# A segment-recurrent attention kernel: mask of the last keys only, token mask by a GpSimd multiply, row sums and selection in 32-column tiles, output projection whole

## The chip, the cores and the metric

One core of one Trainium2 chip. The metric is the device time of one execution in microseconds (us).

## The reference, cut to what matters

The kernel computes `g * a + (1 - g) * b`: `b` is a small MLP that fills gaps and plays no part here, `a` is attention over 64 segments of 32 tokens, each with 8 memory rows that come out of the segment before. That recurrence makes the 64 segments a chain.

```python
M, seg, H, Dh = 8, 32, 32, 128            # memory rows, tokens, heads, head size
idx = jnp.arange(M + seg)
mask = (idx[:, None] < M) | (idx[:, None] >= idx[None, :])   # memory rows see all, token rows are causal
mem = mem0                                                  # [1, 8, 512]
for s in range(64):
    h = concatenate([mem, x[:, 32*s:32*s+32]], axis=1)
    q, k, v = h@Wq, h@Wk, h@Wv                              # per head
    p = softmax(where(mask, q@k.T * scale, -1e9))
    o = (p @ v) @ Wo
    mem = o[:, :M]                                          # goes into the next segment
    outs.append(o[:, M:])
```

Of the kernel before, what the change touches and what calls it, by code (L numbers as in the profile page):

```python
# [23 lines left out]
def kernel(ctx, tc, A_x, A_mem0, A_Wq, A_Wk, A_Wv, A_Wo, A_seg_len, B_x, B_w1, B_b1, B_w2, B_b2, gate_w, out):  # L24
# [46 lines left out]
    MkA = l0.tile([P, 4, EW], BF16)  # L71
# [83 lines left out]
    nc.gpsimd.memset(MkA[:], 0.0)  # L155
    for hh in range(4):
        for g in range(4):
            q = slice(32 * g, 32 * g + 32)
            for (c0, c1) in ((0, M), (EW - LEFT, EW)):
                sl = MkA[q, hh, c0:c1]  # L160
                nc.gpsimd.affine_select(out=sl, in_=sl, pattern=[[0, c1 - c0]], compare_op=ALU.is_ge,
                                        fill=MASK_NEG, base=-LEFT * hh, channel_multiplier=1)
            sl = MkA[q, hh, 0:M]
            nc.gpsimd.affine_select(out=sl, in_=sl, pattern=[[0, M]], compare_op=ALU.is_ge,
                                    fill=MASK_NEG, base=LEFT * hh + LEFT - 1, channel_multiplier=-1)

            sl = MkA[q, hh, EW - LEFT:EW]
            nc.gpsimd.affine_select(out=sl, in_=sl, pattern=[[1, LEFT]], compare_op=ALU.is_ge,
                                    fill=MASK_NEG, base=LEFT * hh, channel_multiplier=-1)

            sl = MkA[q, hh, 2 * M:2 * M + RIDE]
            nc.gpsimd.affine_select(out=sl, in_=sl, pattern=[[1, RIDE]], compare_op=ALU.is_ge,
                                    fill=MASK_NEG, base=M, channel_multiplier=-1)
# [181 lines left out]

    def mask_mm():

        B = bank(7, [P, 512])
        S = B[:, 0:NG * EW].rearrange("p (i e) -> p i e", e=EW)
        nc.tensor.matmul(S, lhsT=ident[:], rhs=MkA[:].unsqueeze(2).to_broadcast([P, 4, 2, EW]),  # L360
                         start=True, stop=True, skip_group_check=True)
        return B, S
# [234 lines left out]
    def run_fill(n):  # L597
        for _ in range(n):
            next(fill, None)
# [21 lines left out]
    for s in range(nseg + 2):  # L621
# [11 lines left out]
        if live:  # L633
            B, S = S_next
            na, nb, nc_, nd, ne = ring
            ring = (nd, ne, na, nc_, nb)
# [28 lines left out]
            for kc in range(1, KC):  # L665
# [5 lines left out]
            nc.scalar.activation(out=E[:, :, 16:EW], in_=S[:, :, 16:EW], func=ACTF.Exp, scale=scale, accum_out=hist[:, s, 1:2])  # L671
            sm = bank(nc_, [P, NG, 8])
            nc.tensor.matmul(sm[:], lhsT=BO[:], rhs=E[:, :, 8:16], start=True, stop=False)  # L673
            nc.tensor.matmul(sm[:], lhsT=BO[:], rhs=E[:, :, 0:8], start=False, stop=True)  # L674
# [4 lines left out]
            nc.vector.tensor_tensor(out=Pm[:].rearrange("p i (a q) -> p i a q", q=8), in0=E[:, :, 0:16].rearrange("p i (a q) -> p i a q", q=8),  # L679
                                    in1=R[:, 0:8 * NG].rearrange("p (i q) -> p i q", q=8).unsqueeze(2).to_broadcast([P, NG, 2, 8]), op=ALU.mult)  # L680
# [3 lines left out]
            nc.tensor.matmul(sr, lhsT=BO[:], rhs=E[:, :, 16:48], start=True, stop=False, skip_group_check=True)  # L684
            nc.tensor.matmul(sr[:, :, 24:32], lhsT=BO[:], rhs=E[:, :, 48:56], start=False, stop=True, skip_group_check=True)
# [4 lines left out]
            run_fill(1)  # L690
        else:
            if s == nseg:
                ux_out(s - 2)
                x_mul(s - 1)
                av_x(s - 1, (ne, na, nc_, 7))
# [5 lines left out]
        for half in range(2):  # L701
            d = slice(256 * half, 256 * half + 256)
            wp = bank((nb, nd)[half], [P, 256])
            for u in range(8):
                wo_unit(wp, UTT[Tp % 2], 24 - 8 * sp, u, 256 * half, 256 * half + 256)
            if half == 0:
                flush(act_q, 2)
            (nc.scalar.copy if half else nc.vector.tensor_copy)(out=wsb[:, d], in_=wp[:])  # L708
# [4 lines left out]
        if live and s >= 1:  # L713
            av_x(s - 1, (ne, na, nc_, nb))
        run_fill(2 * (si == 3))
        if s + 1 < nseg:
            aT = S_next[0][:, NG * EW:NG * EW + KC * M].rearrange("p (k m) -> p k m", m=M)
            for m in range(KC):
                nc.tensor.matmul(aT[:, m, :], lhsT=wsb[:, m * P:(m + 1) * P], rhs=Sel[:, 0:M], start=False, stop=True, skip_group_check=True)  # L719
# [145 lines left out]
```

## The kernel before: the parts that the change and the argument touch

Four segments ("quarters" 0 to 3, `si` in the code) share one 128-row tile of x. A segment has 40 keys: 8 memory rows and 24 tokens fill 32 partitions, and the last 8 tokens are handled as a "left" part for a whole tile at once (`KL`, `VL`, `GL`). The scores of all 32 heads lie in one PSUM bank, 32 partitions for each of four heads.

```python
def mask_mm():                       # adds the mask to the scores' bank ahead of them: 448 columns
    B = bank(7, [P, 512])
    S = B[:, 0:NG * EW].rearrange("p (i e) -> p i e", e=EW)
    nc.tensor.matmul(S, lhsT=ident[:], rhs=MkA[:].unsqueeze(2).to_broadcast([P, 4, 2, EW]), start=True, stop=True, ...)
    return B, S

def prep_h(s): nc.gpsimd.tensor_copy(out=hT[s % NHT][:, :, M:32], in_=xTs[T][...])       # 96 columns
def prep_q(s): nc.gpsimd.tensor_copy(out=QT[:, :, 32:40], in_=QL[T % 2][...])            # 256 columns
def left_v_in(T): nc.gpsimd.tensor_copy(out=VL[T % 2][:], in_=vls.pop(T)[:])             # 1024 columns
def x_mul(s): ...                    # GpSimd: Px = E * R (token rows), racc += R; waits for the second reciprocal

for s in range(nseg + 2):
    if si == 3 and T + 1 < NT: left_v_in(T + 1)
    if si == 3 and T + 2 < NT: x_left(T + 2)              # GL, a GpSimd copy
    ...
    if s + 1 < nseg: prep_h(s + 1)
    if s >= 1:
        prep_q(s)
        x_mul(s - 1)
    # ... projections Q, K, V of this segment (L211, L222), scores ...
    nc.scalar.activation(out=E[:, :, 0:16], in_=S[:, :, 0:16], func=ACTF.Exp, ...)        # memory rows' columns
    nc.scalar.activation(out=E[:, :, 16:EW], in_=S[:, :, 16:EW], func=ACTF.Exp, ...)      # token rows' columns
    sm = bank(nc_, [P, NG, 8])
    nc.tensor.matmul(sm[:], lhsT=BO[:], rhs=E[:, :, 8:16], start=True, stop=False)        # sums, memory rows
    nc.tensor.matmul(sm[:], lhsT=BO[:], rhs=E[:, :, 0:8], start=False, stop=True)
    run_fill(5 + (si == 3))                                                               # side work on TensorE
    nc.vector.reciprocal(out=R[...], in_=sm[:])
    nc.vector.tensor_tensor(out=Pm..., in0=E[:, :, 0:16]..., in1=R..., op=ALU.mult)       # 128 elements
    av(Um, 8, s, V, Pm, 8, 0, 0)                                                          # value product, memory rows
    # ... sums of the token rows (L684, L685), their reciprocal (1.76 us), UTT casts, run_fill(1) ...
    for half in range(2):                                                                 # output projection
        wp = bank((nb, nd)[half], [P, 256])
        for u in range(8):
            wo_unit(wp, UTT[Tp % 2], 24 - 8 * sp, u, 256 * half, 256 * half + 256)
        (nc.scalar.copy if half else nc.vector.tensor_copy)(out=wsb[:, d], in_=wp[:])
    S_next = mask_mm()
    av_x(s - 1, (ne, na, nc_, nb))                                                        # value product, token rows of s-1
    run_fill(2 * (si == 3))
    for m in range(KC):                                                                   # selection of the new memory
        nc.tensor.matmul(aT[:, m, :], lhsT=wsb[:, m * P:(m + 1) * P], rhs=Sel[:, 0:M], start=False, stop=True, ...)
    nc.vector.tensor_copy(out=hn[:, :, 0:M], in_=aT)                                      # memory of the next segment
```

A scheduler may move instructions, but each engine runs its own in one order. The GpSimd copies of `prep_h`, `prep_q`, `left_v_in` and `x_left` stand, in program order, behind everything that the segment before put on GpSimd.

## Time and profile before

| | before |
|---|---|
| time, median of 4 runs | 835.51 us (835.13 to 835.79) |
| loop, first to last memory-row sums | 705.9 us |
| length of a segment, quarters 0 to 3 (medians) | 10.943, 10.996, 11.032, 11.681 us |
| TensorE weight-shape changes in 106 to 811 us | 574, some nine a segment |

A segment's length is taken from the start of its memory-row sums to the next segment's. I read the starts of matmuls throughout, since their ends are modelled and overlap. The waits of TensorE have the columns total us, how many, the longest:

```profile
PEld L384 <- DVE Pm L679: 32.0, 64, 1.6
```

The weight loads of the memory rows' value product wait for the VectorE multiply `Pm`, 64 times, 0.5 us each. PEld is only the loader; most of this lies beside the side matmuls, so it is a figure to compare and not time lost.

### The profile page before, as it was taken

The numbers are of one execution on the slowest core, as the hardware profiler recorded it, in microseconds if no ns is written. First come the engines' busy times: TensorE is split into PE (matmuls) and PEld (weight loads), VectorE is DVE, ScalarE is ACT, GpSimd is POOL, SyncE is SP. The second block draws the span as 40 slices with busy tenths as digits, with TensorE's granted clock in tenths as the row PEclk, the third lists the DMA queues.
The fourth block names the chain that finished last, engine by engine and source line by source line (L and its number), as shares of the span: only waits on it lengthen the run. The fifth ranks groups of instructions, "written<-read, shape, count | busy, mean of one in ns | idle before, by whom it ended". The sixth has DMA issues, their size and how long they took to land.

```text
span 832.9 us, 49239 instructions
## 1 busy us (share of the span) xinstructions
PE 804.7 (97%) x22405; PEld 495.4 (59%) x22417; DVE 501.7 (60%) x1019; ACT 434.0 (52%) x1245; POOL 273.7 (33%) x625
## 2 busy tenths in 40 slices
PE   6999999999999999999999999999999999999886
PEld 4665555665666665566566556656656656665554
DVE  5764256565666566666656565656656665666553
ACT  3555544555455555555554555455555555555552
POOL 8000234242424333332424242434243243424220
PEclk9999999999999999999999999999999999999999
DMA  9791210100000010101010100000010101010000
GB/s 318 253 391 44 87 32 7 28 12 24 15 23 23 17 28 10 37 11 35 10 27 13 35 11 22 23 20 26 12 34 10 36 10 35 5 35 5 10 5 24
DMA packets 38216, 37.64 MB, mean 45 GB/s; under 512 B 13545, under 2 KB 36434, under 8 KB 36466
## 3 DMA queue, kind: packets, MB, share of 16 engines
q1 hardware_dynamic: 37874, 34.31, 12.4%
q8 instruction: 177, 2.90, 1.5%
q14 instruction: 37, 0.30, 0.1%
q0 software_dynamic: 128, 0.13, 0.1%
HBM read 26.03 MB, written 6.29 MB: 39 GB/s over the span
## 4 chain that ended last, share of the span: by engine, by line
PE 93%; DVE 3%; DMA 1%; issue 1%; SPq 1%; ACT 1%; DVEq 0%; ACTq 0%
PE b L211 35%; PE b L233 18%; PE b L222 17%; PE b L384 5%; PE hp L456 4%; PE bp L473 4%; PE b L360 2%; PE b L369 2%; PE b L684 2%; PE b L719 1%; PE b L389 1%; PE b L673 1%; DMA Wo_sb<-in_A_x_dram 1%; PE b L320 1%; PE b L373 0%
## 5 line engine op out<-in xcount | busy, mean ns | idle before, releaser
L217 DVE STREAM_TRANSPOSE Tt<-b 128x512 f32<-128x512 f32 (+1 forms) x384 | 225.6, 613 | 85.5 <-PE b L211 71.8
L211 PEld LDWEIGHTS <-hT 128*32 128x32 bf16 x5120 | 134.7, 97 | 100.0 <-DVE hT L720 15.4
L233 PE MATMUL b<-Wo_sb,UTT 128*32 128x256 bf16 (+1 forms) x4736 | 162.7, 285 | 1.2 <-ACT UTT L619 0.8
L222 PE MATMUL b<-Wv_sb,hT 128*32 128x512 bf16 x2048 | 141.9, 379 | 0.0
L211 PE MATMUL b<-Wq_sb,hT 128*32 128x512 bf16 x2048 | 132.9, 380 | 1.4 <-DVE hT L720 1.4
L211 PE MATMUL b<-Wk_sb,hT 128*32 128x256 bf16 (+1 forms) x3072 | 133.3, 308 | 0.0
L233 PEld LDWEIGHTS <-UTT 128*32 128x32 bf16 x4736 | 121.4, 97 | 19.1 <-ACT UTT L619 1.5
L654 ACT CAST KT<-Tt 128x256 bf16<-128x256 f32 (+1 forms) x192 | 87.1, 476 | 53.6 <-DVE Tt L217 53.6
L605 POOL TENSOR_TENSOR Px<-E,R 128x256 bf16<-128x256 bf16 x64 | 43.0, 672 | 218.7 <-DVE R L689 218.7
L689 DVE RECIPROCAL R<-b 128x256 f32<-128x256 f32 x64 | 112.5, 1757 | 0.0
L654 POOL CAST QT<-Tt 128x512 bf16<-128x512 f32 x64 | 39.1, 611 | 192.6 <-DVE Tt L217 192.6
L619 ACT CAST UTT<-b 128x256 bf16<-128x256 f32 x256 | 76.8, 387 | 23.9 <-PE b L389 23.4
L708 ACT CAST wsb<-b 128x256 bf16<-128x256 f32 x66 | 24.6, 372 | 120.1 <-PE b L233 120.1
L677 DVE RECIPROCAL R<-b 128x64 f32<-128x64 f32 x64 | 35.6, 557 | 79.4 <-PE b L674 79.4
L654 ACT CAST QT<-Tt 128x512 bf16<-128x512 f32 x64 | 39.6, 619 | 66.7 <-DVE Tt L217 66.7
L384 PEld LDWEIGHTS <-V 32*128 32x128 bf16 x4096 | 35.3, 91 | 46.2 <-DVE Pm L679 32.0
L222 PEld LDWEIGHTS <-hT 128*32 128x32 bf16 x2048 | 49.5, 96 | 21.1
L688 ACT CAST UTT<-b 128x64 bf16<-128x64 f32 x128 | 20.9, 215 | 75.2 <-PE b L389 75.2
L461 ACT ACTIVATE hg<-hp,b_sb 128x256 bf16<-128x256 f32 x80 | 37.7, 473 | 38.9 <-PE hp L456 38.9
L456 PE MATMUL hp<-yT,w_sb 128*128 128x256 bf16 (+1 forms) x352 | 53.8, 278 | 2.8 <-ACT hg L461 1.5
L607 POOL TENSOR_TENSOR racc<-racc,R 128x320 f32<-128x320 f32 x64 | 55.5, 867 | 0.0
L720 DVE CAST hT<-b 128x32 bf16<-128x32 f32 x63 | 12.1, 191 | 62.4 <-PE b L719 61.6
(116 smaller groups left out, 1075.2 us busy)
## 6 DMA issues: line engine op xcount, KB each, us to landing
Wv_sb<-in_A_Wv_dram SPq DMA_DIRECT2D x4, 1024.0 KB
Wq_sb<-in_A_Wq_dram SPq DMA_DIRECT2D x4, 1024.0 KB
Wk_sb<-in_A_Wk_dram SPq DMA_DIRECT2D x4, 1024.0 KB
Wo_sb<-in_A_Wo_dram SPq DMA_DIRECT2D x2, 2048.0 KB
vd<-vt SPq DMA_DIRECT2D x32, 128.0 KB
vs<-vd SPq DMA_DIRECT2D x256, 16.0 KB
out_dram<-o SPq DMA_DIRECT2D x16, 128.0 KB
Wo_sb<-in_A_x_dram SPq DMA_DIRECT2D x1, 1024.0 KB
```

The lines of the kernel that those rows point to most:

```text
L211: nc.tensor.matmul(bk[32 * j:32 * j + 32, 0:n], lhsT=G[:, kc, :], rhs=W5[t][:, kc, h0:h1, j, :], start=(kc == 0), stop=(kc == KC - 1), til ...
L217: nc.vector.transpose(out=Tt[:, 0:n], in_=bk[:, 0:n])
L222: nc.tensor.matmul(bk[32 * j:32 * j + 32, :], lhsT=G[:, kc, :], rhs=Wv5[:, kc, 4 * vb:4 * vb + 4, j, :], start=(kc == 0), stop=(kc == KC - ...
L233: nc.tensor.matmul(bk[32 * g:32 * g + 32, :], lhsT=ut[:, i, j, c0:c0 + 32], rhs=Wo_sb[:, 4 * i + j, d0:d1], start=(j == 0 and i < 4), stop ...
L384: nc.tensor.matmul(U[j][:, i, :], lhsT=V[q, i, :], rhs=Pt[q, i, c_main:c_main + n], start=(i == 0), stop=False, skip_group_check=True, til ...
L456: nc.tensor.matmul(hp[:rows, :], lhsT=w1_sb[:, kc, fc * P:fc * P + rows], rhs=yTs[blk][:, kc, :], start=(kc == 0), stop=(kc == KC - 1))
L461: nc.scalar.activation(out=hg_[:rows, :], in_=hp[:rows, :], func=ACTF.Gelu_apprx_tanh, bias=b1_sb[:rows, fc:fc + 1], scale=1.0)
L605: nc.gpsimd.tensor_tensor(out=Px[:, :, 0:32], in0=E[:, :, 16:48], in1=Rr, op=ALU.mult)
L607: nc.gpsimd.tensor_tensor(out=racc[:], in0=racc[:], in1=R[:], op=ALU.add)
L619: nc.scalar.copy(out=UTT[T % 2][:, :, j, c0 + M:c0 + 40], in_=U[:])
L654: (nc.gpsimd.tensor_copy if bi == 2 else nc.scalar.copy)(out=dst, in_=Tv)
L689: nc.vector.reciprocal(out=R[:, 8 * NG:].rearrange("p (i q) -> p i q", q=32), in_=sr)
```

## The change

The intent is to cut TensorE time: the mask matmul covers only the left keys (128 columns instead of 448), the causal mask of the tokens becomes a multiply of E by 0 and 1 on GpSimd, the 128-row sums and the selection become groups of four 32-column tiles (so that TensorE need not change shape between them and the projections), and the output projection runs in one piece of 512 columns, copied by ScalarE alone.

```diff
 def mask_mm():
-        nc.tensor.matmul(S, lhsT=ident[:], rhs=MkA[:].unsqueeze(2).to_broadcast([P, 4, 2, EW]), ...)
+        for j in range(4):
+            q = slice(32 * j, 32 * j + 32)
+            nc.tensor.matmul(S[q].rearrange("p i (a b) -> p i a b", b=LEFT)[:, :, 0:7:6, :], lhsT=ident[:, q], rhs=MkL[:],
+                             ..., tile_position=(0, 32 * j))
+    def sums(o, rhs, start, stop):
+        for j in range(4):
+            q = slice(32 * j, 32 * j + 32)
+            nc.tensor.matmul(o[q], lhsT=BO[:, q], rhs=rhs, start=start, stop=stop, ..., tile_position=(0, 32 * j))
+    def mem_out(aT, wsb):            # the selection, 16 matmuls instead of 4
+        for m in range(KC):
+            for c in range(4): ...   # 32 columns of wsb each, tile_position=(0, 32 * c)
# ... in the loop, after the two exp ...
+            Em = E[:, :, 16:16 + RIDE]
+            nc.gpsimd.tensor_tensor(out=Em, in0=Em, in1=Tri[:].unsqueeze(1).to_broadcast([P, NG, RIDE]), op=ALU.mult)
-            nc.tensor.matmul(sm[:], lhsT=BO[:], rhs=E[:, :, 8:16], start=True, stop=False)
-            nc.tensor.matmul(sm[:], lhsT=BO[:], rhs=E[:, :, 0:8], start=False, stop=True)
+            sums(sm, E[:, :, 8:16], True, False)
+            sums(sm, E[:, :, 0:8], False, True)
-            nc.vector.tensor_tensor(out=Pm..., in0=E[:, :, 0:16]..., in1=R..., op=ALU.mult)
+            for c in (8, 0):
+                nc.vector.tensor_tensor(out=Pm[:, :, c:c + 8], in0=E[:, :, c:c + 8], in1=R..., op=ALU.mult)
# ... token sums likewise by sums(); banks rotated by one; flush(act_q, 2), waiting ScalarE copies, ahead of the projection ...
-        for half in range(2):
-            ... 16 units of 256 columns, first half copied by VectorE, second by ScalarE
+        wp = bank(nb, [P, Dm])
+        for u in range(8):
+            wo_unit(wp, UTT[Tp % 2], 24 - 8 * sp, u)
+        nc.scalar.copy(out=wsb[:], in_=wp[:])
```

More of the change, by code (lines that the diff above doesn't have):

```diff
@@ L70 @@
     VL = [l0.tile([P, SPT, 2, Dh], BF16, name=f"VL{i}") for i in range(2)]
-    MkA = l0.tile([P, 4, EW], BF16)
+    MkL = l0.tile([P, NG, 2, LEFT], BF16)
+    Tri = l0.tile([P, RIDE], BF16)
     BO = l0.tile([P, P], BF16)
@@ L152 @@
         nc.gpsimd.tensor_copy(out=SelL[i][:, RIDE:32], in_=Sel[:, LEFT * (SPT - 1 - i):LEFT * (SPT - i)])
-    nc.gpsimd.memset(MkA[:], 0.0)
-    for hh in range(4):
+    nc.gpsimd.memset(Tri[:], 1.0)
+    for g in range(4):
+        q = slice(32 * g, 32 * g + 32)
+        nc.gpsimd.affine_select(out=Tri[q, :], in_=Tri[q, :], pattern=[[1, RIDE]], compare_op=ALU.is_ge,
+                                fill=0.0, base=M, channel_multiplier=-1)
+    nc.gpsimd.memset(MkL[:], 0.0)
+    for i in range(0, NG, 2):
+        hh = i // 2
         for g in range(4):
             q = slice(32 * g, 32 * g + 32)
-            for (c0, c1) in ((0, M), (EW - LEFT, EW)):
-                sl = MkA[q, hh, c0:c1]
-                nc.gpsimd.affine_select(out=sl, in_=sl, pattern=[[0, c1 - c0]], compare_op=ALU.is_ge,
+            for c in range(2):
+                sl = MkL[q, i, c, :]
+                nc.gpsimd.affine_select(out=sl, in_=sl, pattern=[[0, LEFT]], compare_op=ALU.is_ge,
                                         fill=MASK_NEG, base=-LEFT * hh, channel_multiplier=1)
-            sl = MkA[q, hh, 0:M]
-            nc.gpsimd.affine_select(out=sl, in_=sl, pattern=[[0, M]], compare_op=ALU.is_ge,
+            sl = MkL[q, i, 0, :]
+            nc.gpsimd.affine_select(out=sl, in_=sl, pattern=[[0, LEFT]], compare_op=ALU.is_ge,
                                     fill=MASK_NEG, base=LEFT * hh + LEFT - 1, channel_multiplier=-1)
-            sl = MkA[q, hh, EW - LEFT:EW]
+            sl = MkL[q, i, 1, :]
             nc.gpsimd.affine_select(out=sl, in_=sl, pattern=[[1, LEFT]], compare_op=ALU.is_ge,
                                     fill=MASK_NEG, base=LEFT * hh, channel_multiplier=-1)
-            sl = MkA[q, hh, 2 * M:2 * M + RIDE]
-            nc.gpsimd.affine_select(out=sl, in_=sl, pattern=[[1, RIDE]], compare_op=ALU.is_ge,
-                                    fill=MASK_NEG, base=M, channel_multiplier=-1)
+        nc.gpsimd.tensor_copy(out=MkL[:, i + 1, :, :], in_=MkL[:, i, :, :])
     pools.update(nTt=2, nside=1)
@@ L354, in prep_q @@
         nc.gpsimd.tensor_copy(out=QT[:, :, 32:40], in_=QL[T % 2][:, :, LEFT * si:LEFT * si + LEFT])
+    def sums(o, rhs, start, stop):
+        for j in range(4):
+            q = slice(32 * j, 32 * j + 32)
+            nc.tensor.matmul(o[q], lhsT=BO[:, q], rhs=rhs, start=start, stop=stop, skip_group_check=True, tile_position=(0, 32 * j))
+    def mem_out(aT, wsb):
+        for m in range(KC):
+            for c in range(4):
+                nc.tensor.matmul(aT[32 * c:32 * c + 32, m, :], lhsT=wsb[:, m * P + 32 * c:m * P + 32 * c + 32], rhs=Sel[:, 0:M],
+                                 start=False, stop=True, skip_group_check=True, tile_position=(0, 32 * c))
     def mask_mm():
@@ L359, in mask_mm @@
         S = B[:, 0:NG * EW].rearrange("p (i e) -> p i e", e=EW)
-        nc.tensor.matmul(S, lhsT=ident[:], rhs=MkA[:].unsqueeze(2).to_broadcast([P, 4, 2, EW]),
-                         start=True, stop=True, skip_group_check=True)
+        for j in range(4):
+            q = slice(32 * j, 32 * j + 32)
+            nc.tensor.matmul(S[q].rearrange("p i (a b) -> p i a b", b=LEFT)[:, :, 0:7:6, :], lhsT=ident[:, q], rhs=MkL[:],
+                             start=True, stop=True, skip_group_check=True, tile_position=(0, 32 * j))
         return B, S
@@ L635 @@
             na, nb, nc_, nd, ne = ring
-            ring = (nd, ne, na, nc_, nb)
+            ring = (nb, nd, ne, na, nc_)
             qk_banks = (na, nb, nc_, nd, ne)
@@ L678 @@
             Pm = cw.tile([P, NG, 16], BF16, tag="Pm", bufs=1, name="Pm")
-            nc.vector.tensor_tensor(out=Pm[:].rearrange("p i (a q) -> p i a q", q=8), in0=E[:, :, 0:16].rearrange("p i (a q) -> p i a q", q=8),
-                                    in1=R[:, 0:8 * NG].rearrange("p (i q) -> p i q", q=8).unsqueeze(2).to_broadcast([P, NG, 2, 8]), op=ALU.mult)
+            for c in (8, 0):
+                nc.vector.tensor_tensor(out=Pm[:, :, c:c + 8], in0=E[:, :, c:c + 8], in1=R[:, 0:8 * NG].rearrange("p (i q) -> p i q", q=8), op=ALU.mult)
             Um = [bank(k, [P, NG, 8]) for k in (nd, ne, na, nc_)]
@@ L683 @@
             sr = B[:, 0:NG * 32].rearrange("p (i q) -> p i q", q=32)
-            nc.tensor.matmul(sr, lhsT=BO[:], rhs=E[:, :, 16:48], start=True, stop=False, skip_group_check=True)
-            nc.tensor.matmul(sr[:, :, 24:32], lhsT=BO[:], rhs=E[:, :, 48:56], start=False, stop=True, skip_group_check=True)
+            sums(sr, E[:, :, 16:48], True, False)
+            sums(sr[:, :, 24:32], E[:, :, 48:56], False, True)
             Tp, sp = divmod(s - 2, SPT)
@@ L690 @@
             run_fill(1)
+            flush(act_q, 2)
         else:
@@ L694 @@
                 x_mul(s - 1)
-                av_x(s - 1, (ne, na, nc_, 7))
+                av_x(s - 1, (nd, ne, na, nc_))
             else:
@@ L700 @@
         wsb = cw.tile([P, Dm], BF16, tag="wsb", bufs=9, name="wsb")
-        for half in range(2):
-            d = slice(256 * half, 256 * half + 256)
-            wp = bank((nb, nd)[half], [P, 256])
-            for u in range(8):
-                wo_unit(wp, UTT[Tp % 2], 24 - 8 * sp, u, 256 * half, 256 * half + 256)
-            if half == 0:
-                flush(act_q, 2)
-            (nc.scalar.copy if half else nc.vector.tensor_copy)(out=wsb[:, d], in_=wp[:])
+        wp = bank(nb, [P, Dm])
+        for u in range(8):
+            wo_unit(wp, UTT[Tp % 2], 24 - 8 * sp, u)
+        nc.scalar.copy(out=wsb[:], in_=wp[:])
         if s >= 2:
@@ L713 @@
         if live and s >= 1:
-            av_x(s - 1, (ne, na, nc_, nb))
+            av_x(s - 1, (nd, ne, na, nc_))
         run_fill(2 * (si == 3))
@@ L717 @@
             aT = S_next[0][:, NG * EW:NG * EW + KC * M].rearrange("p (k m) -> p k m", m=M)
-            for m in range(KC):
-                nc.tensor.matmul(aT[:, m, :], lhsT=wsb[:, m * P:(m + 1) * P], rhs=Sel[:, 0:M], start=False, stop=True, skip_group_check=True)
+            mem_out(aT, wsb)
             nc.vector.tensor_copy(out=hn[:, :, 0:M], in_=aT)
```

## The prediction

> **What bounds the kernel now.** I read the page's busy shares first, then its chain, then one segment in order of time. There are 64 segments of 32 tokens. Four of them (called quarters 0 to 3) share one 128-row tile of x.
>
> ```profile
> PE 804.7 (97%) x22405; PEld 495.4 (59%) x22417; DVE 501.7 (60%) x1019; ACT 434.0 (52%) x1245; POOL 273.7 (33%) x625
> PE 93%; DVE 3%; DMA 1%; issue 1%; SPq 1%; ACT 1%; DVEq 0%; ACTq 0%
> ```
>
> TensorE is busy 97% of the span and is 93% of the chain that ended last. In the loop (106 to 811 us) it stands for anything else less than 10 us. So a saving must be a saving of TensorE time, and what it saves it keeps only if no other engine makes it wait. The loop in order of time, TensorE only, in a quarter 0 (start, length):
>
> ```profile
> 509.32 0.82 PE L222 MATMUL b<-Wv_sb,hT 128*32 128x512 bf16 x12
> 510.07 0.20 PE L673 MATMUL b<-E,BO 128*128 128x64 bf16 x1
> 510.11 0.19 PE L674 MATMUL b<-E,BO 128*128 128x64 bf16 x1
> 510.23 1.26 PE L222 MATMUL b<-Wv_sb,GL 128*32 128x512 bf16 x20
> 511.43 0.36 PE L384 MATMUL b<-Pm,V 32*128 32x8 bf16 x32
> 511.64 0.23 PE L389 MATMUL b<-Pm,VL 32*128 32x32 bf16 x8
> 511.81 0.28 PE L684 MATMUL b<-E,BO 128*128 128x256 bf16 x1
> 511.93 0.19 PE L685 MATMUL b<-E,BO 128*128 128x64 bf16 x1
> 512.05 0.40 PE L222 MATMUL b<-Wv_sb,GL 128*32 128x512 bf16 x4
> 512.28 1.92 PE L233 MATMUL b<-Wo_sb,UTT 128*32 128x256 bf16 x64
> 514.13 0.36 PE L360 MATMUL b<-MkA,ident 128*128 128x448 bf16 x1
> 514.42 0.37 PE L384 MATMUL b<-Px,V 32*128 32x32 bf16 x32
> 514.64 0.24 PE L389 MATMUL b<-Px,VL 32*128 32x32 bf16 x8
> ```
>
> Read the starts, not the lengths: lengths overlap. A group of four 128*32 matmuls of 512 columns takes 0.215 us from start to start of the next group, one of 256 columns 0.108. Whenever the weight shape changes (128*32, 128*128, 32*128) the next start comes later than the columns explain: 64 columns at L674 should take 0.027 us, the next start comes after 0.123; the eight columns that end L719 cost 0.096; the last group of L222 costs 0.312 in place of 0.215 before L673. Each change of shape costs about 0.095 to 0.10 us. The trace has 574 such changes in the loop, nine a segment, some 57 us.
>
> **What the Trainium skill says.** "TensorEngine Tiling (Array Packing)", section Key Properties: changing the tiling mode, not just the tile, drains TensorE. The trace agrees, at about 0.10 us each. "TensorE: Matmul & The Clock Gate", section "Wait — 56ns, not 53.3ns?", says starts are never closer than about 25 ns. Here small column-tiled matmuls (L369, 40 columns) start 7 ns apart in the mean, since four tiles run together; I use the 7 ns. "SBUF — State Buffer", section "Who interferes with whom": a VectorE instruction with two SBUF inputs contends with a GpSimd instruction that reads SBUF, and the one issued first blocks the other. The trace agrees (a quarter 2):
>
> ```profile
> 532.16 1.04 POOL L299 COPY VL<-vs 128x1024 bf16<-128x1024 bf16 x1
> 532.94 0.40 DVE L679 TENSOR_TENSOR Pm<-E,R 128x128 bf16<-128x128 bf16 x1
> 511.00 0.29 DVE L679 TENSOR_TENSOR Pm<-E,R 128x128 bf16<-128x128 bf16 x1
> ```
>
> The Pm multiply takes 0.29 us alone, but 0.40 beside the VL copy: it ends 0.14 us after the copy's end at 533.20, so it stood still until then.
>
> **The change part by part**, on TensorE, per segment.
> (a) Sums and selection by 32 columns: L673/674, L684/685 and L719 get the shape of their neighbours. The changes of shape left are the two into and two out of the value products (L384/389): four of nine. Five go (six in quarter 3, where side work stands before L719): about 0.5 us.
> (b) The mask matmul falls from 448 to 128 columns: 320 columns, -0.13 us. L719 becomes 16 matmuls of 7 ns in place of four of 30 ns: nothing.
> (c) The projection whole: 8 groups of 0.215 = 1.72 in place of 16 of 0.108 = 1.74 us: nothing on TensorE. But wsb is now one ScalarE copy of 512 columns, which begins only after the whole projection, where before VectorE took the first half meanwhile.
> (d) GpSimd multiplies E by the token mask: 192 elements. From L605 (256 elements, 0.672 us) and L606 (64, 0.306): 1.9 ns an element over 0.18, so about 0.55 us, estimated.
> (e) Pm in two VectorE instructions of 64 elements; I estimate 0.225 each (0.29 less 64 elements at 1 ns), 0.14 apart in start, as two L688 casts are.
>
> Raw TensorE saving 0.65 to 0.75 us, 45 us in all. Now what stays, wait by wait.
>
> Step 1, ahead of the memory rows' sums. The exp L670 ends 0.18 us before L673 starts; its semaphore comes with the accumulator read, 0.10 later, and 0.045 goes until a matmul starts (from the hT case, L720 to L211). So only 0.036 of the 0.10 is won.
> Step 2, sums to value product: 1.357 us before. After: 0.055 + 5 groups 1.08 + one change 0.10 = 1.235. The VectorE chain: reciprocal starts at 0.26, +0.558, +0.104, +0.225, +0.055 = 1.20. So -0.12.
> Step 3, value product to selection (L384 with Pm to L719): 3.382 before in quarters 0 to 2. After, TensorE alone would need about 2.8. But: the first UTT cast lets the projection start no earlier than 0.79; its last group starts at 2.30; ScalarE starts wsb 0.43 later (before: 0.324 for 256 columns, plus 0.107), takes 0.605 (as L282, 512 columns) and TensorE sees it 0.055 later: 3.39. So nothing is won here: the wait for wsb eats what (a) and (b) give. The mask matmul waits for the reciprocal L689 (it ends 2.554 after the product's start, in the same bank), so at 2.62 in place of 2.455; that is hidden under the wsb wait. In quarter 3 two side units (0.43) stand before the selection: 2.62 + 0.16 + 0.38 + 0.43 = 3.59 against 3.926 before: -0.336.
> Step 4, selection to next projections: 0.628 before; after, the chain hT cast: 0.10 + 0.206 + 0.191 + 0.055 = 0.555. -0.073 (quarter 3: +0.015).
> Sum: quarters 0 to 2 -0.22, quarter 3 -0.477: 48 x 0.22 + 16 x 0.477 = 18.2 us, so 817.5 if nothing else happens.
>
> Step 5, what takes some back. The mask multiply sits on GpSimd from about 0.445 (exp L671 ends 0.273 after the sums' start, +0.17) to 0.995, and GpSimd's next copies, which ran earlier before, queue right behind it. Pm's first half is issued at 0.92, just ahead of the next copy, waits for the multiply's end and finishes near 1.145: harmless. The second half is issued at 1.06, behind that copy. In quarters 0, 1 and 3 the copy is hT's (0.27): second half done by 1.39, needed at 1.5, harmless. In quarter 2 the copy is VL's, 1.04 us: second half done near 2.15, and the left value product, due at 1.525, starts at 2.2. Cost 0.65 us x 15 = 10 us, since the sums, the UTT casts, the projection and wsb all follow it. So 818 + 10 = 827 us, about 1% faster.
>
> **The rivals.**
> R1, TensorE is all that counts: it keeps the 0.65 to 0.75 us, 835.74 - 45 = 791. For it: 97% busy, hardly a wait. Against: wsb's copy of 512 columns is on the way from projection to next segment and was partly hidden before. I give it little.
> R2, no blocking of VectorE by GpSimd, or too short to matter: 817.5. For it: the copy may be issued later than I think. Against: L679 at 0.40 in quarter 2.
> R3, the copy wins the race against Pm's first half too (my margin is 0.02 us, 0.92 against 0.94): quarters 0, 1, 3 lose about 0.16 us each, quarter 2 about 0.9: 817.5 + 7.7 + 13.5 = 839. Against: the order of issue decided at such margins in the trace, and my estimate is on the good side, barely.
> R4, ScalarE late for wsb: it has been idle 1.46 us before L708, so no.
>
> **Range and chances.** R2, the main line and R3 give 817.5, 827 and 839. I weigh them about 3 to 5 to 2 and take 826 as the middle, 812 to 838 as the range. Faster by over 2% needs less than 819.4: R2 with luck, or R1: 0.27. Slower by over 2% needs 852: 0.02. Within 2%: 0.71.
>
> **What would show it.** Right: in the loop, changes of shape fall from nine to four a segment; TensorE waits about 0.3 us for wsb (ScalarE) ahead of the selection in quarters 0 to 2 and not in quarter 3; the mask matmul waits for the reciprocal; TensorE's busy time falls far more than the span; the second Pm multiply in quarter 2 lasts some 1 us and the left value product waits for it. Wrong: no TensorE wait on wsb (then R1), or Pm's halves at 0.22 us in every quarter (R2), or the first half at 0.4 us or more in all quarters (R3). A change of shape that costs nothing, or column-tiled sums that run one after another (four times 0.107 us at the token sums), would upset the sum in (a).

## The result, and the profile after

The changed kernel takes 839.88 us (median of 4 runs, 839.80 to 839.96) against 835.51: the ratio is 1.0053 (95% interval 1.0035 to 1.007). Ratios here are the mean time of one kernel's fast runs over that of the other's fast runs of the same rounds, so not quite the ratio of the medians. It is the same within 2%, and a little slower: outside the predicted range (812 to 838) by 1.9 us, and within 1 us of rival R3 (839).

From the page of the kernel after:

```profile
PE 791.1 (94%) x22021; PEld 444.3 (53%) x22021; DVE 516.6 (62%) x1017; ACT 448.1 (53%) x1245; POOL 305.6 (36%) x682
...
PE 86%; DVE 6%; ACT 4%; issue 1%; DMA 1%; SPq 1%; DVEq 0%; ACTq 0%
```

TensorE's busy time fell by 13.6 us and its share of the chain from 93% to 86%. The changes of weight shape fell from 574 to 250 in the same window, four a segment. By the starts each change that went gives back about 0.10 us, as predicted: from the first sums to the next side matmul 0.162 us before and 0.057 after, from the token sums to the next 0.242 and 0.148. (Busy time counts overlapping records, so it shows less of this.) So the change did to TensorE what it was meant to do, and VectorE took the time back: its share of the chain doubled, and it is busy 14.9 us longer although ScalarE took 24.0 us of `wsb` copies from it. `Pm` alone went from 20.1 to 51.1 us. One quarter 0 of the kernel after in order of time, all engines, cut to the lines that matter (start, length):

```profile
513.74 0.24 PE L366 MATMUL b<-E,BO 128*32 128x64 bf16 x8
...
514.19 0.55 POOL L693 TENSOR_TENSOR E<-E,Tri 128x192 bf16<-128x192 bf16 x1 [1.76 <-ACT E L691]
514.68 0.26 POOL L356 COPY hT<-xT 128x96 bf16<-128x96 bf16 x1
514.70 0.66 DVE L702 TENSOR_TENSOR Pm<-E,R 128x64 bf16<-128x64 bf16 x2
...
515.08 0.36 PE L404 MATMUL b<-Pm,V 32*128 32x8 bf16 x32
...
517.91 0.59 ACT L727 CAST wsb<-b 128x512 bf16<-128x512 f32 x1 [1.39 <-PE b L239]
...
518.55 0.27 PE L371 MATMUL b<-Sel,wsb 128*32 128x8 bf16 x16
```

and a quarter 2:

```profile
535.72 0.24 PE L366 MATMUL b<-E,BO 128*32 128x64 bf16 x8
...
536.66 1.04 POOL L305 COPY VL<-vs 128x1024 bf16<-128x1024 bf16 x1
536.67 1.33 DVE L702 TENSOR_TENSOR Pm<-E,R 128x64 bf16<-128x64 bf16 x2
...
537.83 0.36 PE L404 MATMUL b<-Pm,V 32*128 32x8 bf16 x32 [0.79 <-DVE Pm L702]
```

What to see: in 58 of the 64 segments, in all quarters, a GpSimd copy is recorded 0.012 to 0.022 us before the `Pm` pair by the trace's nanoseconds, and the first half is long. In four others the copy comes 0.06 to 0.10 us after the pair's start, and there the first half takes 0.225 us. The `Pm` pair lasts 0.66 us beside the short hT copy and 1.33 us beside the VL copy. In quarter 2 the value product, 1.34 us after the sums in quarter 0, comes 2.11 us after them, with TensorE standing still for 0.79 us. Columns as in the waits before (total us, how many, longest):

```profile
PEld L404 <- DVE Pm L702: 45.2, 64, 1.3
...
PEld L371 <- ACT wsb L727: 10.8, 50, 0.7
...
PE b L404 <- DVE Pm L702: 16.1, 19, 1.2
```

and the last of them in the kernel before:

```profile
PE b L384 <- DVE Pm L679: 5.7, 6, 1.3
```

The loader's wait for `Pm` grew from 32.0 to 45.2 us, and TensorE itself now stands still for it 16.1 us in 19 segments, where it was 5.7 us in 6. The second line is the predicted wait for the ScalarE copy of `wsb`: 50 of them, for the 48 segments of quarters 0 to 2, some 0.2 us each.

Medians by quarter, from the starts of the matmuls in each trace; "order" is the first experiment below, put here because it is the change without its accident:

| us | quarter | before | after | order |
|---|---|---|---|---|
| segment | 0 | 10.943 | 10.940 | 10.778 |
| | 1 | 10.996 | 10.990 | 10.835 |
| | 2 | 11.032 | 11.691 | 10.835 |
| | 3 | 11.681 | 11.306 | 11.307 |
| sums to value product | 0 | 1.357 | 1.338 | 1.253 |
| | 2 | 1.393 | 2.112 | 1.254 |
| | 3 | 1.573 | 1.470 | 1.469 |
| value product to selection | 0 | 3.383 | 3.467 | 3.391 |
| | 3 | 3.927 | 3.631 | 3.631 |
| selection to next projections | 0 | 0.628 | 0.588 | 0.588 |

After against before: quarters 0 and 1 gain nothing, quarter 2 loses 0.66 us and quarter 3 gains 0.375. Times 16 this is +4.4 us, and the time rose by 4.4. That they agree so well is partly chance: the loop itself rose by 3.6 us (705.9 to 709.5), and the rest lies before it.

### The profile page after: what moved, and what is told of

The parts are those of the page before. It is cut to its first block, busy times and chain, and to the rows that moved or that the text cites. A ratio compares the mean times of both kernels' runs of the same rounds, so it can differ in the third digit from the quotient of the medians.

```text
span 838.2 us, 48544 instructions
## 1 busy us (share of the span) xinstructions
PE 791.1 (94%) x22021; PEld 444.3 (53%) x22021; DVE 516.6 (62%) x1017; ACT 448.1 (53%) x1245; POOL 305.6 (36%) x682
## 4 chain that ended last, share of the span: by engine, by line
PE 86%; DVE 6%; ACT 4%; issue 1%; DMA 1%; SPq 1%; DVEq 0%; ACTq 0%
PE b L217 32%; PE b L239 17%; PE b L228 16%; PE hp L476 4%; PE bp L493 4%; ACT wsb L727 4%; PE b L404 3%; PE b L366 3%; DVE Pm L702 2%; PE b L371 2%; PE b L389 2%; DVE R L699 1%; PE b L409 1%; DMA Wo_sb<-in_A_x_dram 1%; PE b L393 0%
## 5 line engine op out<-in xcount | busy, mean ns | idle before, releaser
L217 PEld LDWEIGHTS <-hT 128*32 128x32 bf16 x5120 | 131.3, 97 | 108.0 <-DVE hT L738 23.6
L239 PE MATMUL b<-Wo_sb,UTT 128*32 128x512 bf16 x2624 | 161.6, 380 | 1.2 <-ACT UTT L639 1.0
L727 ACT CAST wsb<-b 128x512 bf16<-128x512 f32 x66 | 38.7, 586 | 116.6 <-PE b L239 116.6
L239 PEld LDWEIGHTS <-UTT 128*32 128x32 bf16 x2624 | 63.5, 96 | 62.7 <-DVE UTT L710 7.2
L404 PEld LDWEIGHTS <-V 32*128 32x128 bf16 x4096 | 34.9, 91 | 50.7 <-DVE Pm L702 45.2
L228 PEld LDWEIGHTS <-hT 128*32 128x32 bf16 x2048 | 49.4, 96 | 21.2
L693 POOL TENSOR_TENSOR E<-E,Tri 128x192 bf16<-128x192 bf16 x64 | 35.2, 550 | 68.0 <-ACT E L691 68.0
```

The lines of the kernel that those rows point to most:

```text
L217: nc.tensor.matmul(bk[32 * j:32 * j + 32, 0:n], lhsT=G[:, kc, :], rhs=W5[t][:, kc, h0:h1, j, :], start=(kc == 0), stop=(kc == KC - 1), til ...
L228: nc.tensor.matmul(bk[32 * j:32 * j + 32, :], lhsT=G[:, kc, :], rhs=Wv5[:, kc, 4 * vb:4 * vb + 4, j, :], start=(kc == 0), stop=(kc == KC - ...
L239: nc.tensor.matmul(bk[32 * g:32 * g + 32, :], lhsT=ut[:, i, j, c0:c0 + 32], rhs=Wo_sb[:, 4 * i + j, d0:d1], start=(j == 0 and i < 4), stop ...
L404: nc.tensor.matmul(U[j][:, i, :], lhsT=V[q, i, :], rhs=Pt[q, i, c_main:c_main + n], start=(i == 0), stop=False, skip_group_check=True, til ...
L727: nc.scalar.copy(out=wsb[:], in_=wp[:])
```

## The experiments

Theory A: the loss is the lock. A GpSimd copy that queues behind the mask multiply takes the shared read port ahead of VectorE's first `Pm` half. Rival B: the mask multiply itself (its length, its load on GpSimd) costs the time. Rival C: the new forms on TensorE, or the whole projection, cost it. (In the expectations of runs 1 to 4 the letters stand the other way round: their theory C is the load on GpSimd, their theory B is TensorE's new forms.) Twelve runs, all with correct results; each median is quoted with the ratio to the kernel before from the same rounds.

### 1. The copies moved behind the Px multiplies

The same instructions; only the order on GpSimd changes: VL, GL, hT and QT are copied after `Px` of the segment before, long after `Pm`.

```diff
 for s in range(nseg + 2):
-        if si == 3 and T + 1 < NT:
-            left_v_in(T + 1)
-        if si == 3 and T + 2 < NT:
-            x_left(T + 2)
         ...
+            if s >= 1:
+                x_mul(s - 1)
+            if si == 3 and T + 1 < NT:
+                left_v_in(T + 1)
+            if si == 3 and T + 2 < NT:
+                x_left(T + 2)
             if s + 1 < nseg:
                 prep_h(s + 1)
             if s >= 1:
                 prep_q(s)
-                x_mul(s - 1)
```

> The changed kernel with only GpSimd's order altered: the copies of VL, GL, hT and QT come after the Px multiplies instead of right behind the mask multiply. Theory A (a GpSimd copy queued behind the mask multiply holds off the two Pm multiplies of VectorE): both Pm halves take about 0.22 us, the product starts about 1.24 us after the sums in quarters 0 to 2, quarter 2 falls from 11.69 to about 10.8 us and quarters 0 and 1 by about 0.2; 818 us. Theory B (the column tiling or the whole projection does not bring what I counted, and the queue is beside the point): no change, 839. Theory C (GpSimd has simply more work than it can do in time): no change either, the work is the same, 839.

Measured: 823.32 us, ratio 0.9848 (0.9832 to 0.9865), 5 us above the 818 expected from A (the section on the prediction says where they lie). A quarter 0 of it in order of time:

```profile
504.70 0.55 POOL L694 TENSOR_TENSOR E<-E,Tri 128x192 bf16<-128x192 bf16 x1 [1.75 <-ACT E L692]
...
505.21 0.36 DVE L703 TENSOR_TENSOR Pm<-E,R 128x64 bf16<-128x64 bf16 x2
...
508.23 0.67 POOL L625 TENSOR_TENSOR Px<-E,R 128x256 bf16<-128x256 bf16 x1 [2.98 <-DVE R L712]
```

Behind the mask multiply GpSimd now does nothing for 2.98 us, and the `Pm` pair takes 0.36 us. The groups of VectorE instructions show the same over the whole run (busy us and mean ns after the first bar), first the kernel after, then this one:

```profile
L702 DVE TENSOR_TENSOR Pm<-E,R 128x64 bf16<-128x64 bf16 x128 | 51.1, 438 | 7.0 <-DVE R L699 0.5
```

```profile
L703 DVE TENSOR_TENSOR Pm<-E,R 128x64 bf16<-128x64 bf16 x128 | 23.1, 222 | 7.0 <-DVE R L700 0.5
```

```profile
PEld L404 <- DVE Pm L703: 31.2, 64, 1.3
```

One `Pm` half takes 222 ns without a copy beside it and 438 ns in the mean with one. The wait for `Pm` (the last fence, waits of this kernel) is back at 31.2 us. The change without this collision is 1.5% faster than before; the collision costs 839.88 - 823.32 = 16.6 us. A stands. B and C expected 839.

### 2. More work on GpSimd: a useless memset behind the multiply

The order of the change kept, but a memset of 300 columns (0.349 us) put between the mask multiply and the copies.

```diff
+    pad = lp.tile([P, 300], FP32)
             nc.gpsimd.tensor_tensor(out=Em, in0=Em, in1=Tri[...], op=ALU.mult)
+            nc.gpsimd.memset(pad[:], 0.0)
```

> The changed kernel with a useless memset of 300 fp32 columns (about 0.35 us, it reads nothing) on GpSimd between the mask multiply and the copies. Theory A (order of issue): the copies now start some 0.36 us later, behind both Pm multiplies, so Pm runs freely and more GpSimd work makes the kernel faster: 818 to 821. Theory C (GpSimd overloaded): slower than 839, up to 0.35 x 64 = 22 us. Theory B: 839.

Measured: 823.10 us, ratio 0.9847 (0.9831 to 0.9864), 2 us above the range expected. More GpSimd work makes the kernel as fast as run 1: GpSimd's load is not the cause (B falls), the moment at which the copy starts is. The memset reads nothing and does not hold VectorE up: `Pm` halves take 225 ns beside it. The Trainium skill says just that ("SBUF — State Buffer", section "Who interferes with whom": a VectorE instruction with two SBUF inputs contends with a GpSimd instruction that reads SBUF, "not with one that only writes it"), and this run agrees.

### 3. The multiply alone, in the kernel before

```diff
# before.py
+            Em = E[:, :, 16:16 + RIDE]
+            nc.gpsimd.tensor_tensor(out=Em, in0=Em, in1=Tri[...], op=ALU.mult)     # redundant: the mask matmul stays
```

> The kernel before, plus the mask multiply on GpSimd (redundant there, the result stays right), nothing else. Theory A: in quarter 2 the VL copy moves behind the multiply and starts just before Pm, which then ends only about 2.09 us after the sums: +0.75 us x 15 = 11 us, so 847; in quarters 0 and 1 the one Pm waits for the hT copy (0.27) only and ends at 1.31, at the time TensorE needs it anyway: under 0.03 us each; quarter 3 nothing. Theory C (load): the same loss in each quarter. Theory B: 836, no loss, as nothing of the tiling is in it.

Measured: 847.29 us, ratio 1.0139 (1.0118 to 1.0159), as expected. The segments are 10.949, 11.011, 11.781 and 11.680 us: quarters 0, 1 and 3 are those of before (10.943, 10.996, 11.681), and quarter 2 has lost 0.75. The old form has enough spare time ahead of the value product to cover a block of 0.1 us or so, not one by the 1.04 us VL copy. `Pm` of this kernel (mean 315 ns before):

```profile
L687 DVE TENSOR_TENSOR Pm<-E,R 128x128 bf16<-128x128 bf16 x64 | 34.8, 544 | 7.0 <-DVE R L685 0.5
```

### 4. The tiling alone, in the kernel before

Mask, projection and `Pm` as before.

```diff
# before.py
-            nc.tensor.matmul(sm[:], lhsT=BO[:], rhs=E[:, :, 8:16], start=True, stop=False)
-            nc.tensor.matmul(sm[:], lhsT=BO[:], rhs=E[:, :, 0:8], start=False, stop=True)
+            sums(sm, E[:, :, 8:16], True, False)      # and the token sums likewise
+            sums(sm, E[:, :, 0:8], False, True)
-            for m in range(KC):
-                nc.tensor.matmul(aT[:, m, :], lhsT=wsb[:, m * P:(m + 1) * P], rhs=Sel[:, 0:M], ...)
+            mem_out(aT, wsb)
```

> The kernel before with only the sums and the selection in 32-column tiling; mask matmul, halves of the projection and Pm stay as before. Step by step: sums 0.039 earlier, product 0.087 earlier (Pm ends at 1.27), selection 0.077 earlier (0.19 in quarter 3), next projections 0.04 earlier: -0.24 in quarters 0 and 1, -0.12 in quarter 2, -0.28 in quarter 3, together 14 us: 821. Theory B (tiling does not pay): 834 or more.

Measured: 834.64 us, ratio 0.9993 (0.9974 to 1.0013). A miss: I expected 821. To see where it went I took two figures from the matmul starts of each trace. The *undisturbed path* is the 15th percentile of the segments' lengths in each quarter, summed over the four quarters; times 16 it is the loop without accidents. The *stops* are what 52 full segments take beyond their quarter's figure. Here the path is 44.196 us against 44.644 before, 7.2 us over the loop (I had expected 14), and the stops rose from 3.2 to 8.1 us. What these stops are comes after run 9.

### 5. A gap of 0.1 us: the predicted main line made to happen

As run 2, with a memset of 8 columns (0.10 us), so that the first `Pm` half gets ahead of the copy and the second does not.

> The changed kernel with a memset of 8 columns only (about 0.1 us) on GpSimd between the mask multiply and the copies. This moves the race by some 0.07 to 0.1 us: the next copy now starts behind the first Pm multiply but ahead of the second. Theory A, which is the main line of the prediction made true: the first half runs freely (0.22 us) in all quarters, the second is held by the hT copy in quarters 0 and 1 (harmless) and by the VL copy in quarter 2, whose left value product comes some 0.7 us late: 823 + 10 = 833 us. If theory A is wrong about the order of issue, it stays at 839.

Measured: 832.34 us, ratio 0.9958 (0.9941 to 0.9975), as expected. A quarter 0 in order of time:

```profile
510.59 0.10 POOL L695 MEMSET pad<- 128x8 f32 x1
510.61 0.43 DVE L704 TENSOR_TENSOR Pm<-E,R 128x64 bf16<-128x64 bf16 x2
510.64 0.32 POOL L356 COPY hT<-xT 128x96 bf16<-128x96 bf16 x1
```

Now the copy comes 0.02 to 0.03 us after the start of the first half (0.024 in the median), and the first half runs at 0.225 us; only the second is held, 0.284 us in quarters 0 and 1 and 1.058 in quarter 2. Quarters 0, 1 and 3 are then as in run 1 (10.780, 10.832, 11.303), and quarter 2 alone is long, 11.528. This is the main line of the prediction's step 5. It would have held if the copy had come some 0.04 us later against `Pm`.

### 6. The mask by a matmul of 448 columns in tiles, no multiply

```diff
-            nc.tensor.matmul(S[q]...[:, :, 0:7:6, :], lhsT=ident[:, q], rhs=MkL[:], ...)
+            nc.tensor.matmul(S[q], lhsT=ident[:, q], rhs=MkA[:].unsqueeze(2).to_broadcast([P, 4, 2, EW]), ...)
-            nc.gpsimd.tensor_tensor(out=Em, in0=Em, in1=Tri[...], op=ALU.mult)
```

> The changed kernel with only its mask part undone: all mask columns by the mask matmul (448 columns, four 32-column tiles side by side), no multiply on GpSimd. Theory A: quarters 0 and 1 as with the other order of GpSimd (10.78 and 10.84 us), since the 0.13 us more of mask matmul hide under the wait for wsb; quarter 2 loses about 0.3 (VL's copy ends after Pm is issued, as in the kernel before, and GL's holds the second half), quarter 3 loses 0.12 against 11.31: 829 us. A theory that the mask matmul's width is what matters: 0.13 x 64 = 8 us over e1 in all quarters alike, 831, with quarter 0 at 10.9.

Measured: 825.71 us, ratio 0.988 (0.9864 to 0.9897), 3 to 5 us faster than either theory had it: a miss. Without the multiply the copies do not collide outside quarter 2 (`Pm` 246 ns in the mean), although they stand in the order of the change. Against run 1 the path is (43.994 - 43.749) x 16 = 3.9 us longer. Some 2.1 us of it lie in quarter 3 (11.440 against 11.307), where no wait for `wsb` hides the longer mask: that is what the shorter mask is worth. The other 1.8 us lie in quarter 2 (10.946 against 10.835), where the VL copy still holds the first half (0.35 us) and the GL copy the second (0.31).

### 7 and 8. Run 1 with the projection in halves again; and then the token value product ahead of the mask too

```diff
# run 7, on run 1
-        wp = bank(nb, [P, Dm])
-        for u in range(8):
-            wo_unit(wp, UTT[Tp % 2], 24 - 8 * sp, u)
-        nc.scalar.copy(out=wsb[:], in_=wp[:])
+        for half in range(2):
+            d = slice(256 * half, 256 * half + 256)
+            wp = bank((nc_ if live else 7, nb)[half], [P, 256])
+            for u in range(8):
+                wo_unit(wp, UTT[Tp % 2], 24 - 8 * sp, u, 256 * half, 256 * half + 256)
+            (nc.scalar.copy if half else nc.vector.tensor_copy)(out=wsb[:, d], in_=wp[:])
# run 8, on run 7: S_next = mask_mm() moved behind av_x(s - 1, ...) and run_fill
```

> e1's order, and the projection again in two halves of 256 columns, VectorE copying the first half of wsb, ScalarE the second. By the steps the selection in quarters 0 to 2 then starts 3.2 us after the product in place of 3.39: -0.18 x 48 = -9 us, so 815 if TensorE's 64 more instructions a segment cost nothing. Rival: e4, with halves too, showed stops of 0.2 to 0.7 us between small matmuls that wait for no semaphore; if these come from the number of instructions they come back here and cost some 5 us: 819.

> e7, and the value product of the token rows (with quarter 3's side units) placed ahead of the mask matmul, so that the mask's wait for the reciprocal hides under it: quarter 3 -0.1 us, the others at most -0.03 as wsb is next to bind: 813 to 818.

Measured: run 7 834.28 us, ratio 0.9991 (0.9971 to 1.001); run 8 834.30 us, ratio 0.9975 (0.9956 to 0.9994). Both miss, by 15 to 21 us. The halves shorten the way from value product to selection as expected (3.268 against 3.391), but the next projections then come 0.65 after the selection instead of 0.588: in all the path gains 0.07 us in four segments. And the stops are 11.1 and 12.6 us, against 1.8 in run 1. One of them, TensorE only, in run 7:

```profile
168.16 0.45 PE L404 MATMUL b<-Px,V 32*128 32x32 bf16 x32
168.46 0.18 PE L409 MATMUL b<-Px,VL 32*128 32x32 bf16 x4
169.55 0.19 PE L409 MATMUL b<-Px,VL 32*128 32x32 bf16 x4 [0.92 <-issue]
```

TensorE stands still for 0.92 us in the middle of a group of eight equal matmuls, and "issue" means that it waits for nothing that the profile shows. The waits of run 7 list such stops by line; the costliest of matmuls is below (3.2 us in five). In the kernel before, all such lines of matmuls come to 0.7 us.

```profile
PE b L409 <- issue: 3.2, 5, 0.9
```

### 9. Run 1 with 32 useless small matmuls a segment

To ask whether it is the number of instructions: ahead of the mask matmul, 32 matmuls of 8 columns into the mask's own bank, which the mask then overwrites. So 366 matmuls a segment, as in run 7.

```diff
 def mask_mm():
+        for _ in range(8):
+            for j in range(4):
+                q = slice(32 * j, 32 * j + 32)
+                nc.tensor.matmul(S[q, 0, 0:8], lhsT=ident[:, q], rhs=MkL[:, 0, 0, :], ..., tile_position=(0, 32 * j))
```

> e1 with 32 more useless matmuls of 8 columns ahead of the mask matmul in each segment (same place, same bank, the result stays right): as many more instructions as the split projection has, nothing else of it. By the columns and 7 ns each they take 0.22 us, which hides under the wait for wsb in quarters 0 to 2 (+0.02) and shows in quarter 3 (+0.22): 823.3 + 4.5 = 828. If TensorE stops for want of instructions (the theory for e4 and e7), stops of 0.2 to 1 us without a semaphore come back in a good part of the segments: 834 or more.

Measured: 834.88 us, ratio 1.0002 (0.9986 to 1.0019). The time is that of the theory of missing instructions, but not for its reason: the path grew by (44.224 - 43.749) x 16 = 7.6 us, where I had expected 4.5 (quarters 0 to 2 lose 0.07 to 0.12 us each, 0.06 of it between the selection and the next projections, 0.646 against 0.588 in quarters 1 and 2; no run here says why), and the stops rose only from 1.8 to 4.7 us. The number of matmuls and the stops side by side:

| kernel | matmuls a segment | path, us | stops, us (52 segments) | segments with a stop over 0.1 us | time, us |
|---|---|---|---|---|---|
| run 12 (before, projection whole) | 307 | 44.799 | 0.6 | 2 | 835.73 |
| before | 339 | 44.644 | 3.2 | 9 | 835.51 |
| after | 334 | 44.888 | 2.1 | 6 | 839.88 |
| run 1 (order) | 334 | 43.749 | 1.8 | 5 | 823.32 |
| run 4 (tiling alone) | 363 | 44.196 | 8.1 | 18 | 834.64 |
| run 7 (order, halves) | 366 | 43.683 | 11.1 | 21 | 834.28 |
| run 8 (run 7, token product first) | 366 | 43.791 | 12.6 | 24 | 834.30 |
| run 9 (run 1 + 32 matmuls) | 366 | 44.224 | 4.7 | 18 | 834.88 |

The page's DMA queue of instructions (packets, MB, share) before and in run 7:

```profile
q8 instruction: 177, 2.90, 1.5%
```

```profile
q8 instruction: 190, 3.11, 1.6%
```

The bytes of this queue (16 KB a packet) come to 64.5 to 64.7 for each matmul and weight load of TensorE in all of the seven traces that I compared (the table's without run 8), so they seem to be TensorE's own instructions. And the stops keep time with them: in the loops of the table's kernels 61 matmuls have a stop put down to "issue", and each of the 61 starts 1.2 to 1.6 us after the last packet before it has landed, though a packet comes only about every 4 us. So TensorE seems to run out of instructions where many short matmuls follow one another. The runs show that the stops go with the number of matmuls and with the packets; the mechanism itself is not proven, and run 9 gave less than half the stops of run 7 at the same number, so where the matmuls stand matters too. It has little part in the verdict on the change: before and after have nearly the same number (339 and 334), and the stops fell by 1.1 us.

### 10. Run 1 with the token value product ahead of the mask, projection whole

```diff
-        if s + 1 < nseg:
-            S_next = mask_mm()
         if live and s >= 1:
             av_x(s - 1, (nd, ne, na, nc_))
         run_fill(2 * (si == 3))
         if s + 1 < nseg:
+            S_next = mask_mm()
             aT = ...
```

> e1 with the token rows' value product and quarter 3's side units ahead of the mask matmul, the projection whole. Quarter 3: the wait of the mask for the reciprocal hides, -0.1 us x 16 = -1.6 us; quarters 0 to 2 stay bound by wsb: 821.7. If the mask's wait mattered in the other quarters too: 819.

Measured: 820.62 us, ratio 0.9827 (0.981 to 0.9843), the fastest version. TensorE from the end of the projection, in order of time:

```profile
506.45 0.37 PE L404 MATMUL b<-Px,V 32*128 32x32 bf16 x32
506.67 0.24 PE L409 MATMUL b<-Px,VL 32*128 32x32 bf16 x8
506.84 0.24 PE L380 MATMUL b<-MkL,ident 128*32 128x128 bf16 x4
```

The value product does not need the reciprocal for which the mask waits, so it fills that time; quarter 3, with side work there and no wait for `wsb`, falls from 11.307 to 11.194 us.

### 11. `Pm` in one instruction

```diff
# after.py
-            for c in (8, 0):
-                nc.vector.tensor_tensor(out=Pm[:, :, c:c + 8], in0=E[:, :, c:c + 8], in1=R..., op=ALU.mult)
+            nc.vector.tensor_tensor(out=Pm..., in0=E[:, :, 0:16]..., in1=R..., op=ALU.mult)
```

> The changed kernel with Pm in one instruction again. Theory A: one wait for GpSimd's copy in place of two; quarters 0 and 1: the product 0.03 later, the left product no more held (-0.12), so -0.05 us net after the wsb wait; quarter 2 unchanged within 0.03. 838.5. If the split of Pm were the cause of the loss: 823 to 828.

Measured: 838.84 us, ratio 1.0045 (1.0028 to 1.0061), as expected. One blocked instruction of 128 elements (typically 0.39 us, mean 0.536) or two of 64: no difference of weight, and the two halves are not the cause.

### 12. The whole projection alone, in the kernel before

```diff
# before.py
-        for half in range(2): ...                     # 16 units of 256 columns, two copies
+        wp = bank(nb, [P, Dm])
+        for u in range(8):
+            wo_unit(wp, UTT[Tp % 2], 24 - 8 * sp, u)
+        nc.scalar.copy(out=wsb[:], in_=wp[:])         # banks and flush(act_q, 2) as in the change
```

> The kernel before with only the projection whole (and the ring of banks that goes with it). By the steps the selection waits for the one wsb copy: +0.05 us in quarters 0 to 2, 2.5 us; fewer instructions take away the 2 us of stops that I count in the trace of the kernel before: 836, same. If the number of instructions costs more than I count there: 830.

Measured: 835.73 us, ratio 1.0008 (0.9991 to 1.0025), as expected. The way from value product to selection grows by 0.057 us in quarters 0 to 2 (one ScalarE copy of 512 columns in place of two of 256 on two engines), and the stops nearly vanish with 307 matmuls a segment. With run 4, rival C is answered: neither TensorE part slows the kernel by itself.

## Why the prediction was wrong

The mechanism was named, its outcome not. The prediction said 826 and gave the outcome that came (R3, 839) a weight of about 2 in 10.

**The step that failed** is in step 5: "Pm's first half is issued at 0.92, just ahead of the next copy". Both times count from the start of the memory rows' sums. The copy came when the prediction had it: 0.941 measured, 0.94 predicted. The multiply came late, at 0.957. The term that was mis-sized is the start of the reciprocal ahead of it: 0.26 in step 2, 0.295 measured. It was 0.269 in the kernel before and is 0.294 in run 4, where only the sums and the selection are tiled: the tiled sums themselves cost the 0.025 us. The rest of the chain (0.558 and 0.104 us) was right. So the copy is recorded 0.012 to 0.022 us ahead of the multiply; I had it 0.02 behind, a margin smaller than the errors of the terms.

Records alone do not settle such an order: the Trainium skill, "Perfetto Trace Analysis", section "Summary: the profiler window per engine type", says that a VectorE row leaves out the start of the prefetch. Lengths settle it here: the first half takes 0.321 us or more with the copy recorded ahead of it, and 0.225 when no copy is there (run 1) or when it comes 0.02 us after the multiply (run 5). With a margin like that, 2 in 10 was too little for R3, and a range whose top lay 1 us under R3's value was too narrow.

| step, as predicted | measured (run 1 for steps 1 to 4) |
|---|---|
| 1: sums 0.036 us earlier | 0.039 (0.312 to 0.273): right |
| 2: sums to value product 1.235 | 1.253: right |
| 3: value product to selection 3.39, `wsb` eats the gain; quarter 3 3.59 | 3.391 with waits for `wsb`; quarter 3 3.631: right, 0.04 too good in quarter 3 |
| 3: mask matmul waits for the reciprocal, at 2.62 | 2.633: right |
| 4: selection to projections 0.555; quarter 3 +0.015 | 0.588; quarter 3 +0.066: 0.03 and 0.05 short |
| sum of steps 1 to 4: -18.2 us | path (44.644 - 43.749) x 16 = -14.3 us |
| 5, mask multiply about 0.55 us | 0.55 us: right |
| 5: the first half ahead of the copy, only quarter 2 loses, 0.65 | true only with the gap of run 5: quarter 2 there 0.69 over run 1 |
| R3: quarters 0, 1, 3 lose 0.16 each, quarter 2 0.9 | quarters 0, 1, 3: 0.162, 0.155, 0.00; quarter 2: 0.856 (after less run 1) |

So steps 1 to 3 hold to some hundredths, step 4 was 0.03 to 0.05 us a segment too good, and the size of each block in R3 was right but for quarter 3: there six side units instead of five stand between sums and value product, and the product comes no later than in run 1 (1.470 and 1.469 us after the sums). That R3's 839 falls so near the 839.88 is partly luck. Its base was 5.8 us too low (823.3 in run 1 against 817.5): 3.9 us from the sum of steps, the rest from the stretches before and after the loop, which I had taken as unchanged; the profiled runs show the loop starting at 106 to 107.9 us, varying from run to run, and some 0.8 us more behind it. And its blocks were too high (21.2 us predicted over that base, 16.6 measured).

R1 (791) is refuted: five changes of shape fewer a segment did not carry through, since `wsb`'s copy and the VectorE chain take their place. R2's case without blocking is run 1: 823, not 817.5.

**Where the gain of the TensorE part went**, then: of the 0.65 to 0.75 us a segment that the prediction estimated for TensorE, 0.22 stay in run 1 (14.3 us over 64 segments), the rest turns into waits for the exp's semaphore, the VectorE chain and the ScalarE copy of `wsb`; and the order of GpSimd's queue takes 16.6 us back.

## What to carry to other kernels

When work is added to an in-order engine, ask what queues behind it and at which moment that now starts, not only how long the added work lasts: here the copies that used to run early moved onto the one VectorE multiply on the critical path, and a mere change of their order was worth 2%. Where an estimate turns on which of two instructions comes first by hundredths of a us, treat it as a coin and spread the range over both outcomes, or fix the order in the program. Before cutting TensorE time, find the waits that will take its place; before splitting matmuls into more and shorter ones, count them, since in these runs the split forms (runs 4 and 7) lost to stops most of what they had saved, or more.

## What the Trainium skill lacked or had wrong

- "TensorEngine Tiling (Array Packing)", section Key Properties, has the drain at a change of tiling mode but no size: 0.095 to 0.10 us each here, with 574 changes before and 250 after.
- "TensorE: Matmul & The Clock Gate", section "Wait — 56ns, not 53.3ns?", puts a floor of about 25 ns on the distance of starts, and does not say there that it leaves out tiles. Column-tiled matmuls that run four at a time start about 7 ns apart in the mean here (6.6 in the selection), so the floor does not hold across tiles. The same page's part on row and column tiling does have starts some 4 ns apart for tiles.
- "SBUF — State Buffer", section "Who interferes with whom", was right on whom and on the exclusive lock, but lacks what a queue of GpSimd copies does: the next copy is recorded 0.055 to 0.06 us before the one ahead of it ends, and blocks a VectorE multiply recorded 0.012 to 0.022 us after it. The waiting VectorE instruction gets its turn after that one copy, not after the whole queue (first `Pm` half 0.325 us beside the hT copy, second then held by the QT copy, 0.416).
- "Trainium Architecture — The Big Picture", section "The software stack", says that the instruction streams are moved into each engine's memory when the program is loaded. In these traces a queue of instructions moves packets of 16 KB all through the run (177 before, 190 in run 7). "Runtime: NRT & Kernel Launch", section "Instruction fetch mechanics", has this right: it tells of refills in blocks of that size during the run.
- That section of the Runtime page takes the refill to be hidden in straight code, and no page has a cost for it. Here stops of 0.2 to 0.9 us with no semaphore follow the packets, 1.8 us in all with 334 matmuls a segment and 11.1 with 366 (runs 1 and 7). That it is the supply of instructions is likely and not proven.
